# Two-bank exp groups and a third shared PSUM bank in the opening of an attention and gated-MLP block

## The chip, the cores and the metric

The kernel runs on one core of one Trainium2 chip. The metric is the device time in microseconds of one launch. Before the change the median of three runs is 854.6 us (853.17 to 856.5); the profiled execution has a span of 849.3 us from its first to its last instruction. A core has five engines that run their own instruction streams and meet at semaphores: TensorE (PE in the profile), VectorE (DVE), ScalarE (ACT), GpSimd (POOL) and SyncE (SP), which here issues the transfers. Matmul results go to PSUM, eight banks of 128 partitions by 512 float32 values.

## What is computed

One transformer block with conditioning, batch 1, 2048 tokens, width 640, 32 heads of 20, hidden width 1536, in bfloat16:

```python
mod = (silu(c) @ w_mod).reshape(1, 6, 1, 640)
sa, ca, ga, sb, cb, gb = (mod[:, i] for i in range(6))
h = layernorm(x) * (1 + ca) + sa
q, k, v = heads(h @ wqkv)                          # 32 heads of 20
p = softmax(q @ k.T * 20 ** -0.5)                  # 32 x 2048 x 2048
x = x + ga * ((p @ v).merge_heads() @ wo)
h = layernorm(x) * (1 + cb) + sb
x = x + gb * (((h @ w_gate) * (h @ w_up)) @ w_down)
```

The 32 × 2048 × 2048 exponentials of the softmax are the bulk of the work that isn't matmul.

## The kernel before

The program is laid out by a list scheduler that runs in Python when the kernel is built. Tasks have an engine, a modelled duration, dependencies and a priority; a PSUM bank or a buffer is taken from a pool (`Slots`) when a task starts and given back when its last user starts. The order that comes out is fixed, and is emitted with semaphore waits. The numbers that steer it (gates, leads, reserves) are constants at the top of the file; nothing is scheduled on the chip itself.

**Heads and score blocks.** Heads are treated in 8 sets of 4. With the queries of one chunk (512, 512, 512, 256 or 256 tokens), a set makes an *item*. A *block* is one head, 128 keys by 512 queries (or two key tiles by 256): one PSUM bank of scores, transposed, keys on partitions. In the first chunk an item has 64 blocks. A block goes one of two ways:

- most blocks go to ScalarE, which reads two or three banks in one exp instruction;
- about one in five goes to VectorE ("D" blocks), which makes the exponential from the bit pattern of the number, four blocks at a time: one instruction per block out of PSUM (line 1244), then three on all four (lines 1272, 1277, 1280).

The ScalarE blocks are numbered in one row and cut into groups that alternate between two bank sets, so that the matmuls of one group run while ScalarE reads the other:

```python
while ap < NA:
    even = len(glist) % 2 == 0
    us = ubuf[ap:ap + (3 if even else 2)]
    apos.append(ap)
    ap += len(us)
    glist.append((us, 0 if even else 3))        # banks 0,1,2 or 3,4
...
def fexp(e, nu=nu, b0=b0, cellp=cellp, g=g):    # line 1220
    return e.activation(PPs[g % 2][:, cellp["p"], 0:nu * 512],
                        ps[:, b0:b0 + nu, :].rearrange("p b c -> p (b c)"), AFT.Exp, scale=ESCALE)
```

**PSUM.** Banks 0 to 4 hold the scores of the two group sets; bank 7 sums probability times value (PV). Banks 5 and 6 are the shared pool `G`: every transpose, every projection, every matmul of the output projection and of the MLP, and every D block takes a bank there and keeps it until VectorE or ScalarE has copied it out. Before the first scores, the score banks are lent:

```python
G = Slots([5, 6], "G")
GX = Slots([2, 3, 4], "GX")        # three of the first five transposes
GC = Slots([0, 1], "GC")           # the first two columns of the modulation, fillers
BPV = 7
```

**The opening.** Tokens come in four blocks `tc` of 512. Each block is normalised by VectorE, transposed and scaled into `hT[tc]`, then projected. A head takes 20 rows, but a set's four heads must lie on partitions 0, 32, 64 and 96. There are two ways to get there:

- *direct* (`kq_round`): five times four matmuls of 32 columns put each head on its place, and one copy fills `KT[:, j, ...]`; one round per head set;
- *packed* (`packed_round`): 128 rows of K or Q at a time, a copy to a staging tile, a write to DRAM, and one read of 32 KB per head (K), or one of a whole set (Q), which spreads the rows. Five rounds of 128 rows cover all eight sets.

```python
K_DIRECT = (0, 1)      # head set 0 direct for these token blocks
K_ALL = (0, 1)         # all head sets direct for these token blocks
...
def k_base(tc):
    return 80 if tc in K_DIRECT else 0
def nblk(tc):
    return -(-(D - k_base(tc)) // 128)
...
for tc in range(4):
    if tc > 0 and tc in K_DIRECT:
        kq_round("K", 0, tc, need(tc / 4))
    for t in range(4 * tc, 4 * tc + 4):
        v_round(t, 0, need(t / 16 + V_L))
...
for tc in range(4):
    for j in range(1, NSET if tc in K_ALL else 0):
        late.append((j + tc / 4 - KD_LEAD, 2560, lambda p, g, ...: kq_round("K", j, tc, p, g)))
    for b in range(0 if tc in K_ALL else nblk(tc)):
        r0 = b * 128 + k_base(tc)
        j0 = max(0 if tc not in K_DIRECT else 1, -(-(r0 - 91) // 80))
        late.append((j0 + tc / 4 - K_LEAD, 2560, lambda p, g, ...: packed_round("K", b, tc, p, g)))
```

**Copies out of PSUM.** An `evac` task belongs to VectorE, but ScalarE may take it until `STEAL_END` nanoseconds of model time, when it has no task of its own due within 0.3 us.

**Exp results** go to two rings `PPs` of four slots each, from which PV matmuls read. D blocks join a score group where a row strip of the array is free: a score matmul uses 32 rows, so up to four heads run side by side, and with three blocks in a group one strip is left (`d_attach`). `D_RES` says how far ahead of a due D block projections leave a shared bank to it. The gates of the later projections and of the MLP are counted in exp groups.

Of the kernel before, what the change touches and what calls it, by code (L numbers as in the profile page):

```python
# [21 lines left out]
T0 = 700.0  # L22
DMA_SLOW = 0.0015
DMA_LAT = 1700.0
STEAL_END = 60000.0
STEAL_GAP = 300.0
HAM_W = 3413.3
HAM_MIN = 2550.0
# [37 lines left out]
class Slots:  # L66

    def __init__(self, ids, name=""):
        self.name = name
        self.free = [(i, []) for i in ids]  # L70
        self.hold = {}

    def avail(self, only=None):
        best = None
# [7 lines left out]
                best = (t, k)  # L82
        return best

    def take(self, k, refs=1):
        i, rel = self.free.pop(k)
        self.hold[i] = [refs, []]
        return i, rel

    def done(self, i, task):  # L90
        h = self.hold[i]
        h[0] -= 1
        h[1] = [x for x in h[1] if x.nbytes or x.eng != task.eng] + [task]
        if h[0] == 0:
            del self.hold[i]
            self.free.append((i, h[1]))

    def add(self, i, rel):
        self.free.append((i, rel))
# [289 lines left out]
QUADS = [(3, 3, 3, 3, 3, 3, 4, 3), 3, (3, 3, 3, 3, 3, 3, 4, 3), (1, 2, 1, 2, 1, 2, 0, 2), 1]  # L389
D_LEAD = 0.35  # L390
NB0, NSS = 2, 3
NPS = 4
TS_4X, TT_2X = 600.0, 1145.0
WM_GATE = 16
WM_NEED = 1.802
K_DIRECT = (0, 1)
Q_DIRECT = 2
K_LEAD = 0.577
K_ALL = (0, 1)
KD_LEAD = 0.431  # L400
DMA_WINDOW = 900000
D_LATE = 12
D_RES = 100
PVMIN, PVMAX, PVCAP = 2, 11, 16
GATE_F = [0.8, 0.95, 0.819, 0.5, 1.0]
FILL_MIN = 4200.0
DUP_MIN = 0.0
XN_POOL = ()
# [4 lines left out]
HT_L = 0.072  # L413
V_L = 0
LATE_A = 1.174
LATE_L = 2.08
LATEQ = (3,)
LATEQ_A = 6
LATEQ_F = 0.73
QUAD_GAIN = 0.597233983857778  # L420
NTERM = 2
# [6 lines left out]
def sb_cost(n, rate):  # L428
    return n * rate + 62.0


def build_kernel(nc, A_x, A_wqkv, A_wo, B_x, B_w_gate, B_w_up, B_w_down, c, w_mod, out):
# [166 lines left out]
            stx.append(C.alloc("stx", [128, 2, KD, 128], BF16))  # L599
        nsq, nsx = nsx, len(stx)  # L600

    G = Slots([5, 6], "G")
    GX = Slots([2, 3, 4], "GX")
    GC = Slots([0, 1], "GC")
    BPV = 7
    setA = Slots([0], "A")
# [14 lines left out]
    def dve(dur, f, deps=(), prio=3.0, **k):  # L621
        return sc.add(Task("dve", dur, f, deps, prio=prio, **k))
# [6 lines left out]
    def pool(dur, f, deps=(), prio=3.0, **k):  # L629
        return sc.add(Task("pool", dur, f, deps, prio=prio, **k))  # L630

    def act(dur, f, deps=(), prio=3.0, **k):
        return sc.add(Task("act", dur, f, deps, prio=prio, **k))
# [111 lines left out]
            self.evac = after(self)  # L745
            self.evac[-1].on_start = lambda task: banks.done(b["b"], task)

    def quarters(n, lhs, rhs, st, sp):
        def one(x):
            return lambda e, b: e.matmul(ps[32 * x:32 * x + 32, b, 0:n], lhs()[:, 32 * x:32 * x + 32], rhs(),  # L750
                                         tile_position=(0, 32 * x), start=st, stop=sp, skip_group_check=True)
        return [one(x) for x in range(4)]

# [2 lines left out]
    def X(n):  # L756
        return max(n / 2.4 + 3.0, 60.0)
# [67 lines left out]
    def hT_rounds(tc, prio):  # L825
        s2 = tc % 2
        t_hT[tc] = []
        tr_last[tc] = []
        for k in range(KD):
            mms = []  # L830
            for i in range(4):
                f = lambda e, b, i=i, k=k: e.transpose(bankh(b)[:, i * 128:(i + 1) * 128],  # L832
                                                       xn[:, s2, i, k * 128:(k + 1) * 128], ident[:])
                mms.append((C128, f))

            def after(r, k=k):
                dst = hT[tc][:, k, :]
                fa = lambda e: e.activation(dst, bankh(r.b["b"])[:, 0:512], AFT.Identity,  # L838
                                            bias=mcol[:, 0, k:k + 1], scale=mcol[:, 1, k:k + 1])
                f = lambda e: e.tensor_scalar(dst, bankh(r.b["b"])[:, 0:512], mcol[:, 1, k:k + 1], mcol[:, 0, k:k + 1],  # L840
                                              op0=ALU.mult, op1=ALU.add)
                return [evac(512, 455, f, fa, [r.last] + ev_col)]
            r = Round(mms, [t_xn[tc][i] for i in range(4)] + [p_id], after, prio, name=f"hT{tc}.{k}",
                      banks=GX if tc == 0 and k in (1, 3, 4) else None)
            t_hT[tc].append(r.evac[0])
            tr_last[tc].append(r.last)

# [208 lines left out]
    ap = 0  # L1056
    apos = []
    while ap < NA:
        even = len(glist) % 2 == 0
        us = ubuf[ap:ap + (3 if even else 2)]  # L1060
        apos.append(ap)
        ap += len(us)
        glist.append((us, 0 if even else 3))
# [126 lines left out]

    score_q = []
    act_tasks = []
    gx_evac = [t_hT[0][k] for k in (1, 3, 4)]
    act_of = {}
    st_pv = {"item": 0, "free": [d_pz]}
    d_state = {}
# [122 lines left out]
    def item_end_tasks(it):  # L1319
        ci, j = items[it]  # L1320
        n = CHUNKS[ci][1]
        nb32 = n // 32
        slot = ci % 2
        cell = {}
        t1 = Task("dve", n * 1.1 + 70, lambda e: e.transpose(OT[:, 0:n], ps[:, BPV, 0:n]), [], prio=0.0, name=f"T1.{it}")  # L1325
        t1.acq = [(sOT, "o", 1)]
        item_info[it]["t1"] = t1
        t2 = dve(155, lambda e: e.reciprocal(invT[:, 0:nb32].unsqueeze(2),
                                            OT[:, 0:n].rearrange("p (b c) -> p b c", c=32)[:, :, 0:1]), [t1], prio=1.5)
        t3 = dve(sb_cost(n, 1.04), lambda e: e.tensor_tensor(  # L1330
            OTn[:, 0:n].rearrange("p (b c) -> p b c", c=32), OT[:, 0:n].rearrange("p (b c) -> p b c", c=32),
            invT[:, 0:nb32].unsqueeze(2).to_broadcast([128, nb32, 32]), ALU.mult), [t2], prio=1.5)
        t4 = dve(n * 1.1 + 65, lambda e: e.transpose(OcT[:, cell["s"], 0:n], OTn[:, 0:n]), [t3], prio=1.5)
        pcs = oc_pieces(j) if j < NSET - 1 else []
        t4.acq = [(sOcT, "s", max(1, len(pcs)))]

        def on4(task):
            cell["s"] = task.slots["s"]
            sOT.done(0, task)
        t4.on_start = on4  # L1340
        dms = []
        for (b5, s, r0, nr, ro) in pcs:
            def f(e, b5=b5, s=s, r0=r0, nr=nr, ro=ro):
                return e.dma_start(Ocp[r0:r0 + nr, slot, b5, 0:n],
                                   OcT[32 * s + 1 + ro:32 * s + 1 + ro + nr, cell["s"], 0:n])
            dps = [t4] + ([z_oc[slot]] if b5 == KD - 1 else [])
            if ci >= 2:
                dps += oc_free[ci - 2]
            else:
                dps += [x for l in tr_last.values() for x in l]  # L1350
            t = dma("sp", nr * n * 2, f, dps, prio=2, dur=720.0)
            t.on_start = lambda task: sOcT.done(cell["s"], task)
            dms.append(t)
        oc_ready.setdefault(ci, []).extend(dms)
        if j == NSET - 1:
            oc_ready[ci].append(t4)
            oc_last[ci] = cell
        sc.left += 1
        t1.seq = 0
        return t1  # L1360
# [5 lines left out]
    def suffix(ci):  # L1366
# [88 lines left out]
        for fc in range(FT):  # L1455
            use_x = tail and fc < nsx
            wbuf, dm = [], []
            for w_, wv in enumerate((wgv, wuv)):
# [15 lines left out]
                wbuf.append(cell)  # L1474
                dm.append(t)
            gs = fc % 2
            for w_ in range(2):
                mms = []
                for k in range(KD):
# [63 lines left out]
    def acquire_ready(task, t):  # L1543
        for d in task.deps:
            if d.done is None or d.done + SEM > t:
                return False
        return sc.acquire(task, t)
# [132 lines left out]
            st_pv["item"] += 1  # L1680

    tail_added = [False]

    def d_wants():
        g = pvstate["sidx"]
# [77 lines left out]
    def pick_pe(t):  # L1763
        sc.pull("pe")
        g = pvstate["sidx"]
        if g < NG:
            ts, us = score_q[g]
            if acquire_ready(ts, t):
                start = mode_start("S", t)
                rows = {}  # L1770
                for u in us:
                    rows[u.s] = rows.get(u.s, 0) + 1
                d_attach(ts, t, apos[g], rows, 2, False)
                dur = 216.0 * max(rows.values()) * clk()
                area = 128.0 * sum(rows.values())
                if sc.recent(t) + area < DUP_MIN and sc.free_at["act"] > start + 2 * dur + 100:
                    ts.emits = ts.emits + ts.emits
                    dur *= 2
                    area *= 2
                    sc.ndup += 1  # L1780
                sc.activity(start, area)
                sc.finish_issue(ts, start, dur)
                pvstate["sidx"] += 1
                just_s[0] = True
                sc.pe_mode = "S"
                sc.pe_end = start + dur
                sc.free_at["pe"] = sc.pe_end
                return True
# [14 lines left out]
        elif not tail_added[0]:  # L1803
            tail_added[0] = True
            la = [a for a in act_tasks[-2:]]
            if all(a.done is not None for a in la):
                for b in range(5):
                    G.add(b, la)
            else:
                tail_added[0] = False  # L1810
        if sc.recent(t) < FILL_MIN and ring() >= RINGLOW and pick_x(t):
            return True
        if XFIRST and ring() >= XFIRST and pick_x(t):
            just_s[0] = False
            return True
        cands = pv_candidates(t, PVCAP)
        it = st_pv["item"]
# [100 lines left out]
```

The softmax here doesn't subtract the row's maximum and nothing guards it: scores larger than these inputs give would overflow.

## Time and profile before

| what | value |
|---|---|
| time, median of three | 854.6 us |
| span of the profiled run | 849.3 us |
| first exp starts, last exp ends | 17.46 us, 814.0 us |
| exp instructions | 335 of three banks (mean 1523 ns), 335 of two banks (mean 1101 ns) |
| D blocks, first instruction | 372, 682 ns each, on VectorE |
| PE, DVE, ACT busy | 793.9, 719.6, 778.7 us |
| granted TensorE clock, whole run | 0.982 |

How to read it. "Busy" is the time in which an engine has an instruction in execution; matmuls overlap in the array, so a busy TensorE is not TensorE at its peak, and the durations of overlapping matmuls add up to more than their busy time. A group line names the source line, the engine and operation, what is written from what with shapes, the count, then busy time and the mean of one, and after the last bar the idle time just before such instructions with what ended it. In an order-of-time listing, consecutive alike instructions are merged (x5), and the first shape stands for all; the note in brackets is the idle time ahead and its releaser. "Clock" is the share of full TensorE speed that was granted. Idle time of an engine that is not the bound costs nothing.

### The profile page before, as it was taken

The numbers are of one execution on the slowest core, as the hardware profiler recorded it, in microseconds if no ns is written. First come the engines' busy times: TensorE is split into PE (matmuls) and PEld (weight loads), VectorE is DVE, ScalarE is ACT, GpSimd is POOL, SyncE is SP. The second block draws the span as 40 slices with busy tenths as digits, with TensorE's granted clock in tenths as the row PEclk, the third lists the DMA queues.
The fourth block names the chain that finished last, engine by engine and source line by source line (L and its number), as shares of the span: only waits on it lengthen the run. The fifth ranks groups of instructions, "written<-read, shape, count | busy, mean of one in ns | idle before, by whom it ended". The sixth has DMA issues, their size and how long they took to land.

```text
span 849.3 us, 28015 instructions
## 1 busy us (share of the span) xinstructions
PE 793.9 (93%) x12239; PEld 306.9 (36%) x12239; DVE 719.6 (85%) x1271; ACT 778.7 (92%) x700; POOL 30.6 (4%) x65
## 2 busy tenths in 40 slices
PE   8899999999998999999989999998999999999898
PEld 4432333322223222223323223232344443454477
DVE  7769988899999989898889999889789979677773
ACT  4568899999999999999999999999999999999931
POOL 2300000000001000000001000000011000000000
PEclk9989999999999999999999999999999999999999
DMA  9135222012240122310210122000300236115420
GB/s 296 37 97 158 61 68 58 7 44 76 75 124 18 33 60 57 109 57 13 68 40 6 24 65 56 14 12 14 70 33 6 59 76 135 38 46 113 105 59 20
DMA packets 114433, 53.19 MB, mean 63 GB/s; under 512 B 83359, under 2 KB 114311, under 8 KB 114311
## 3 DMA queue, kind: packets, MB, share of 16 engines
q1 hardware_dynamic: 113383, 50.25, 23.2%
q8 instruction: 97, 1.59, 0.8%
q10 hardware_dynamic: 928, 1.15, 0.4%
q14 instruction: 25, 0.20, 0.1%
HBM read 41.09 MB, written 7.99 MB: 58 GB/s over the span
## 4 chain that ended last, share of the span: by engine, by line
PE 38%; ACT 35%; DVE 16%; issue 11%; POOL 0%; ACTq 0%; DVEq 0%
ACT PP L1220 34%; PE ps_all L750 14%; PE ps_all L1186 11%; PE ps_all L1616 8%; DVE DB L1244 5%; DVE DSS L1277 2%; PE ps_all L917 1%; DVE st L805 1%; DVE DSS L1272 1%; DVE st L1420 1%; DVE xck L1410 1%; PE ps_all L832 1%; DVE wd L1174 1%; PE ps_all L1845 1%; DVE OT L1325 1%
## 5 line engine op out<-in xcount | busy, mean ns | idle before, releaser
L1220 ACT ACTIVATE PP<-ps_all 128x1536 bf16<-128x1536 f32 (+1 forms) x671 | 763.0, 1311 | 17.3 <-PE ps_all L1186 14.7
L1186 PE MATMUL ps_all<-QT,KT 32*128 32x512 bf16 (+1 forms) x2560 | 311.9, 342 | 32.1 <-ACT PP L1220 25.0
L1244 DVE TENSOR_SCALAR DB<-ps_all 128x512 int16<-128x512 f32 x372 | 250.4, 682 | 60.8 <-PE ps_all L1186 59.0
L1186 PEld LDWEIGHTS ps_all<-QT,KT 32*128 32x128 bf16 x2560 | 82.3, 91 | 269.8 <-ACT PP L1220 189.4
L1616 PE MATMUL ps_all<-PP,Vf 128*32 128x512 bf16 (+2 forms) x2112 | 166.3, 347 | 0.4 <-DVE OT L1325 0.2
L1277 DVE TENSOR_TENSOR DSS<-DB,DSS 128x2048 bf16<-128x2048 bf16 x93 | 112.2, 1207 | 0.0
L750 PE MATMUL ps_all<-h2T,stg 128*32 128x512 bf16 x1440 | 109.8, 382 | 1.2 <-DVE DB L1244 0.6
L1616 PEld LDWEIGHTS ps_all<-PP,Vf 128*32 128x32 bf16 (+1 forms) x2112 | 48.1, 94 | 87.9 <-issue 78.2
L1616 PE MATMUL ps_all<-DSS,Vf 128*32 128x512 bf16 (+2 forms) x896 | 75.5, 348 | 0.3 <-DVE DSS L1280 0.2
L1280 DVE TENSOR_SCALAR DSS<-DB 128x2048 int16<-128x2048 int16 x93 | 63.3, 681 | 2.1 <-PE ps_all L1616 2.1
L1272 DVE TENSOR_SCALAR DSS<-DB 128x2048 int16<-128x2048 int16 x93 | 63.3, 681 | 1.6
L750 PE MATMUL ps_all<-wd,hprod 128*32 128x320 bf16 x1152 | 56.2, 302 | 1.2 <-DVE DB L1244 0.7
L750 PEld LDWEIGHTS ps_all<-h2T,stg 128*32 128x32 bf16 x1440 | 33.2, 95 | 37.4 <-issue 15.4
L750 PE MATMUL ps_all<-wo,Ocp 128*32 128x320 bf16 x640 | 34.1, 301 | 1.5 <-DVE DB L1244 1.1
L750 PEld LDWEIGHTS ps_all<-wd,hprod 128*32 128x32 bf16 x1152 | 27.1, 96 | 20.6 <-issue 10.2
L1485 DVE CAST gsb<-ps_all 128x512 bf16<-128x512 f32 (+1 forms) x48 | 29.5, 614 | 3.9 <-PE ps_all L750 3.7
L1325 DVE STREAM_TRANSPOSE OT<-ps_all 128x512 f32<-128x512 f32 (+1 forms) x40 | 24.2, 605 | 10.1 <-PE ps_all L1616 9.8
L917 PE MATMUL ps_all<-hT,wq 128*32 128x512 bf16 x375 | 29.8, 395 | 2.1 <-DVE DB L1244 0.9
L1423 POOL TENSOR_SCALAR sd<-mv 128x1 f32<-128x1 f32 x14 | 6.3, 446 | 707.0 <-DVE mv L1422 707.0
L1616 PEld LDWEIGHTS ps_all<-DSS,Vf 128*32 128x32 bf16 (+1 forms) x896 | 24.5, 96 | 19.2 <-issue 8.0
L750 PE MATMUL ps_all<-wV,hT 128*32 128x320 bf16 x640 | 29.9, 312 | 0.9 <-ACT hT L838 0.3
L1496 DVE TENSOR_TENSOR hprod<-ps_all,gsb 128x512 bf16<-128x512 f32 x36 | 24.6, 683 | 5.4 <-PE ps_all L750 5.1
(108 smaller groups left out, 518.8 us busy)
## 6 DMA issues: line engine op xcount, KB each, us to landing
stg<-in_B_w_gate_dram SPq DMA_DIRECT2D x50, 160.0 KB, 2.5
stg<-in_B_w_up_dram SPq DMA_DIRECT2D x50, 160.0 KB
QT<-q_rows SPq DMA_DIRECT2D x22, 128.0 KB, 2.4
wm<-in_w_mod_dram SPq DMA_DIRECT2D x3, 800.0 KB
x<-in_A_x_dram SPq DMA_DIRECT2D x7, 320.0 KB
KT<-k_rows SPq DMA_DIRECT2D x64, 32.0 KB, 1.9
xck<-in_A_x_dram SPq DMA_DIRECT2D x3, 640.0 KB, 4.2
wd<-in_B_w_down_dram SPq DMA_DIRECT2D x1, 1920.0 KB
```

Of the source, the lines that this page charges most:

```text
L750: return lambda e, b: e.matmul(ps[32 * x:32 * x + 32, b, 0:n], lhs()[:, 32 * x:32 * x + 32], rhs(), tile_position=(0, 32 * x), start=st, s ...
L917: f = [lambda e, b_, k=k, x=x: e.matmul(ps[x:x + min(32, w - x), b_, :], wx[:, k, r0 + x:r0 + min(x + 32, w)], hT[tc][:, k, :], tile_posit ...
L1186: ems.append(lambda e, i=i, kt=kt: e.matmul(dstf()[:, i * u.n:(i + 1) * u.n], KT[32 * u.s:32 * u.s + 32, u.j, kt * 128:(kt + 1) * 128], QT ...
L1220: return e.activation(PPs[g % 2][:, cellp["p"], 0:nu * 512], ps[:, b0:b0 + nu, :].rearrange("p b c -> p (b c)"), AFT.Exp, scale=ESCALE)
L1244: return e.tensor_scalar(DB0[:, st_["slot"], x * 512:(x + 1) * 512], bank(cell["b"]), EBIAS, 0.0, op0=ALU.add, op1=ALU.max)
L1272: return e.tensor_scalar(DSS[:, st_["ss"][0], :], DB0[:, st_["slot"], :], 0x7F, 0x3F00, op0=ALU.bitwise_and, op1=ALU.bitwise_or)
L1277: return e.tensor_tensor(d, DB0[:, st_["slot"], :].bitcast(BF16), d, ALU.mult)
L1280: return e.tensor_scalar(DSS[:, st_["ss"][1], :], DB0[:, st_["slot"], :], 0x7F80, 2, op0=ALU.bitwise_and, op1=ALU.bitwise_or)
L1325: t1 = Task("dve", n * 1.1 + 70, lambda e: e.transpose(OT[:, 0:n], ps[:, BPV, 0:n]), [], prio=0.0, name=f"T1.{it}")
L1485: f = lambda e: e.tensor_copy(gsb[:, gs, 0:n], ps[:, r.b["b"], 0:n])
L1496: f = lambda e: e.tensor_tensor(hprod[:, fc, 0:n], ps[:, r.b["b"], 0:n], gsb[:, gs, 0:n], ALU.mult)
L1616: ems.append(lambda e, i=i, kt=kt, stt=stt, stp=stp: e.matmul(ps[32 * s:32 * s + mc, BPV, 0:u.n], Vf[:, (kt * H + 4 * u.j + s) * VW:(kt * ...
```

## The change

It has four parts.

1. *The first 60 exp groups take two banks each* (banks 0, 1 and banks 3, 4). Later groups alternate three and two as before.
2. *Bank 2 joins the shared pool* `G` until group 59 has been issued; then it is retired from the pool, and group 60 waits for its last user. During the opening, transposes, projections and D blocks have three banks.
3. *K of head set 0 is direct for all four token blocks.* The packed blocks of tokens 1024 to 2047 begin at row 80; there are still five of them.
4. *The plan is refitted*: ScalarE may take copies until 94.9 us in place of 60, and leads, gates, the reserve for D blocks and the limit of PV blocks in one turn have other values.

Three more switches come with it and are off (`GU_ONE`, `XCONT`, `T3_POOL`); they change nothing.

```diff
-STEAL_END = 60000.0
+STEAL_END = 94936.728
@@ class Slots
+    def retire(self, i):
+        self.gone.add(i)
+        for k, (j, rel) in enumerate(self.free):
+            if j == i:
+                self.out[i] = self.free.pop(k)[1]
+                break
@@ in done()
-            self.free.append((i, h[1]))
+            if i in self.gone:
+                self.out[i] = h[1]
+            else:
+                self.free.append((i, h[1]))
@@ constants
+HEADG = 60
+HEAD_OUT = 1
-WM_GATE = 16
-WM_NEED = 1.802
-K_DIRECT = (0, 1)
+WM_GATE = 18
+WM_NEED = 1.721
+K_DIRECT = (0, 1, 2, 3)
-K_LEAD = 0.577
+K_LEAD = 0.567
-KD_LEAD = 0.431
+KD_LEAD = 0.559
-D_RES = 100
-PVMIN, PVMAX, PVCAP = 2, 11, 16
-GATE_F = [0.8, 0.95, 0.819, 0.5, 1.0]
+D_RES = 92
+PVMIN, PVMAX, PVCAP = 2, 11, 18
+GATE_F = [0.8, 0.893, 0.938, 0.5, 1.0]
-LATE_L = 2.08
+LATE_L = 2.164
-LATEQ_A = 6
+LATEQ_A = 7
@@ PSUM
-    G = Slots([5, 6], "G")
-    GX = Slots([2, 3, 4], "GX")
+    G = Slots([5, 6, 2] if HEADG else [5, 6], "G")
+    GX = Slots([3, 4] if HEADG else [2, 3, 4], "GX")
+    hx = (1, 3) if HEADG else (1, 3, 4)
...
@@ groups
-        us = ubuf[ap:ap + (3 if even else 2)]
+        us = ubuf[ap:ap + (3 if even and len(glist) >= HEADG else 2)]
@@ pick_pe
+        if HEADG and g >= HEADG - HEAD_OUT and 2 not in G.gone:
+            G.retire(2)
         if g < NG:
             ts, us = score_q[g]
-            if acquire_ready(ts, t):
+            if HEADG and g == HEADG and 2 in G.out:
+                ts.deps = ts.deps + G.out.pop(2)
+                back[0] = True
+            if (g != HEADG or not HEADG or back[0]) and acquire_ready(ts, t):
...
```

More of the change, by code (lines that the diff above doesn't have):

```diff
@@ L71, in __init__ @@
         self.hold = {}
+        self.gone = set()
+        self.out = {}
     def avail(self, only=None):
@@ L391 @@
 NB0, NSS = 2, 3
+HEADG = 60
+GU_ONE = 0
+XCONT = 0
+T3_POOL = 0
+HEAD_OUT = 1
 NPS = 4
 TS_4X, TT_2X = 600.0, 1145.0
-WM_GATE = 16
-WM_NEED = 1.802
-K_DIRECT = (0, 1)
+WM_GATE = 18
+WM_NEED = 1.721
+K_DIRECT = (0, 1, 2, 3)
 Q_DIRECT = 2
-K_LEAD = 0.577
+K_LEAD = 0.567
 K_ALL = (0, 1)
-KD_LEAD = 0.431
+KD_LEAD = 0.559
 DMA_WINDOW = 900000
 D_LATE = 12
-D_RES = 100
-PVMIN, PVMAX, PVCAP = 2, 11, 16
-GATE_F = [0.8, 0.95, 0.819, 0.5, 1.0]
+D_RES = 92
+PVMIN, PVMAX, PVCAP = 2, 11, 18
+GATE_F = [0.8, 0.893, 0.938, 0.5, 1.0]
 FILL_MIN = 4200.0
@@ L746, in __init__, with quarters @@
             self.evac[-1].on_start = lambda task: banks.done(b["b"], task)
-    def quarters(n, lhs, rhs, st, sp):
+    def quarters(n, lhs, rhs, st, sp, c0=0):
         def one(x):
-            return lambda e, b: e.matmul(ps[32 * x:32 * x + 32, b, 0:n], lhs()[:, 32 * x:32 * x + 32], rhs(),
+            return lambda e, b: e.matmul(ps[32 * x:32 * x + 32, b, c0:c0 + n], lhs()[:, 32 * x:32 * x + 32], rhs(),
                                          tile_position=(0, 32 * x), start=st, stop=sp, skip_group_check=True)
@@ L843, in hT_rounds @@
             r = Round(mms, [t_xn[tc][i] for i in range(4)] + [p_id], after, prio, name=f"hT{tc}.{k}",
-                      banks=GX if tc == 0 and k in (1, 3, 4) else None)
+                      banks=GX if tc == 0 and k in hx else None)
             t_hT[tc].append(r.evac[0])
@@ L1192, in build_kernel @@
     act_tasks = []
-    gx_evac = [t_hT[0][k] for k in (1, 3, 4)]
+    gx_evac = [t_hT[0][k] for k in hx]
     act_of = {}
@@ L1329, in item_end_tasks @@
                                             OT[:, 0:n].rearrange("p (b c) -> p b c", c=32)[:, :, 0:1]), [t1], prio=1.5)
-        t3 = dve(sb_cost(n, 1.04), lambda e: e.tensor_tensor(
+        f3 = lambda e: e.tensor_tensor(
             OTn[:, 0:n].rearrange("p (b c) -> p b c", c=32), OT[:, 0:n].rearrange("p (b c) -> p b c", c=32),
-            invT[:, 0:nb32].unsqueeze(2).to_broadcast([128, nb32, 32]), ALU.mult), [t2], prio=1.5)
+            invT[:, 0:nb32].unsqueeze(2).to_broadcast([128, nb32, 32]), ALU.mult)
+        if T3_POOL and it < len(items) - 1:
+            t3 = pool(n * 2.2 + 200, f3, [t2], prio=0)
+        else:
+            t3 = dve(sb_cost(n, 1.04), f3, [t2], prio=1.5)
         t4 = dve(n * 1.1 + 65, lambda e: e.transpose(OcT[:, cell["s"], 0:n], OTn[:, 0:n]), [t3], prio=1.5)
@@ L1476, in suffix, with after, off @@
             gs = fc % 2
+            if n <= 256 and GU_ONE:
+                mms = []
+                for w_ in range(2):
+                    for k in range(KD):
+                        f = quarters(n, lambda k=k, cell=wbuf[w_]: cell["t"][:, k, :], lambda k=k: h2T[:, k, 0:n],
+                                     k == 0, k == KD - 1, w_ * n)
+                        mms.append((X(n), f))
+                def after(r, gs=gs, fc=fc):
+                    f = lambda e: e.tensor_copy(gsb[:, gs, 0:n], ps[:, r.b["b"], 0:n])
+                    fa = lambda e: e.copy(gsb[:, gs, 0:n], ps[:, r.b["b"], 0:n])
+                    ds = [r.last] + ([g_use[gs]] if gs in g_use else []) + sc_use
+                    if tail:
+                        eg = act(n / 1.2 + 60, fa, ds, prio=1e6)
+                    else:
+                        eg = evac(n, ps_cost(n), f, fa, ds)
+                    f = lambda e: e.tensor_tensor(hprod[:, fc, 0:n], ps[:, r.b["b"], n:2 * n], gsb[:, gs, 0:n], ALU.mult)
+                    return [eg, dve(ps_cost(n), f, [r.last, eg] + (first if alt else bd.get("hp", []) + proj_early + kv_last), prio=1)]
+                r = Round(mms, t_h2 + dm + sfx_done.get("ul", []), after, pr(), gate=gate(2 * KD * n), name=f"u{ci}.{fc}")
+                g_use[gs] = r.evac[1]
+                hp.append(r.evac[1])
+                u_last.append(r.last)
+                if not use_x:
+                    def off(task, wbuf=wbuf):
+                        for w_ in range(2):
+                            sStg[w_].done(wbuf[w_]["i"], task)
+                    r.last.on_start = off
+                continue
             for w_ in range(2):
@@ L1682, in build_kernel @@
     tail_added = [False]
+    back = [False]
     def d_wants():
@@ L1807, in pick_pe @@
                 for b in range(5):
-                    G.add(b, la)
+                    if b != 2 or not HEADG or back[0]:
+                        G.add(b, la)
             else:
@@ L1814, in pick_pe @@
             just_s[0] = False
+            return True
+        if XCONT and xcur[0] is not None and ring() >= XCONT and pick_x(t):
             return True
```

## The prediction, made before the changed kernel was run

> **What bounds the kernel now.** I read the page's engine totals and slices first, then the exp instructions alone by stretch, then all engines in the same stretches, and last the order of time around the one long hole. The totals and the 40 slices of 21.2 us:
>
> ```profile
> PE 793.9 (93%) x12239; PEld 306.9 (36%) x12239; DVE 719.6 (85%) x1271; ACT 778.7 (92%) x700; POOL 30.6 (4%) x65
> ACT  4568899999999999999999999999999999999931
> PEclk9989999999999999999999999999999999999999
> ```
>
> ScalarE (ACT) is full from the sixth slice to the end of the exps. Only the first five slices, some 100 us, and the last two show it below 9. Busy time of the exp line alone, by stretch (columns: from:to in us, length, busy us and count, then clock, DMA share, GB/s):
>
> ```profile
> 17.46:36.00 18.54, 10.72 (x9) 0.95 0.32 90
> 36.00:47.30 11.30, 0.00 (x0) 0.92 0.09 25
> 47.30:60.00 12.70, 10.43 (x9) 0.79 0.48 152
> 60.00:80.00 20.00, 15.14 (x14) 0.87 0.52 154
> 80.00:103.00 23.00, 20.61 (x20) 1.00 0.23 57
> 103.00:814.00 711.00, 706.13 (x622) 0.99 0.22 55
> ```
>
> The first exp starts at 17.46 us and the last ends at 814.0. From 103 us on only 711.0 − 706.1 = 4.9 us are not exp. Before that, 85.5 us of time hold 56.9 us of exp, so 28.6 us are missing. That sum is the whole prize of any change to the opening. ScalarE's other work there (copies out of PSUM) is about 6.2 us, from the engine's 63.1 us busy in all; real idle time is about 22.4 us. The same stretches for all engines (busy us and count of PE, PE weight loads, DVE, ACT, POOL):
>
> ```profile
> 36.00:47.30 11.30, 9.98 (x189) 5.80 (x185) 5.98 (x11) 2.33 (x3) 0.99 (x2) 0.92 0.09 25
> ...
> 80.00:103.00 23.00, 21.85 (x320) 8.89 (x320) 22.56 (x41) 20.61 (x20) 0.00 (x0) 1.00 0.23 57
> ```
>
> In the hole TensorE is busy with projections while both exp-side engines are half empty: a matter of order and latency. By 80 us TensorE (21.9 of 23.0) and VectorE (22.6) are both nearly full, so there a gain needs less work or better packing. What the hole waits for, in order of time (start, length, engine, line):
>
> ```profile
> 29.72 6.12 ACT L1220 ACTIVATE PP<-ps_all 128x1536 bf16<-128x1536 f32 x5 [0.17 <-PE ps_all L1186]
> 39.45 0.69 DVE L926 CAST KPA<-ps_all 128x512 bf16<-128x512 f32 x1 [0.59 <-PE ps_all L917]
> 40.17 0.36 SPq L960 DMA_DIRECT2D k_rows<-KPA  x1
> 41.91 1.71 SPq L973 DMA_DIRECT2D KT<-k_rows  x4
> 47.35 5.59 ACT L1220 ACTIVATE PP<-ps_all 128x1024 bf16<-128x1024 f32 x5 [2.77 <-PE ps_all L1186]
> 47.35 0.34 SPq L960 DMA_DIRECT2D k_rows<-KPA  x1
> 49.51 1.70 SPq L973 DMA_DIRECT2D KT<-k_rows  x4
> ```
>
> Exps stop at 35.84 us, because the K of tokens 0 to 1023 is used up, and start again at 47.35, when K of tokens 1024 to 1535 has been projected, copied out of PSUM at 40.1 us, written to DRAM, read back in four pieces and used for scores at 46.9. From copy to scores is 6.8 us. The same round trip for the last 512 tokens starts at 47.35 and ends in the wait ahead of the exp of 54.36 us (1.42 us in the order of time).
>
> **What the Trainium skill says.** "DMA: Bandwidth & Descriptors", section "Latency and other measured facts", lays most of a transfer's fixed cost of about 2 us on the receipt from memory. This agrees: k_rows<-KPA lands 1.7 us after issue and KT<-k_rows 1.9 us (medians of the DMA issues), and this chain has two in series. "ScalarE: Activation LUTs", "Rules for kernel authors", budgets about 0.3 us per ACTIVATE plus 0.83 ns per element. The trace has two exp forms:
>
> ```profile
> L1220 ACT ACTIVATE PP<-ps_all 128x1536 bf16<-128x1536 f32 x335 | 510.3, 1523 | 12.0 <-PE ps_all L1186 9.4 <-PE ps_all L1616 2.1
> L1220 ACT ACTIVATE PP<-ps_all 128x1024 bf16<-128x1024 f32 x335 | 368.9, 1101 | 5.3 <-PE ps_all L1186 5.3
> ```
>
> A third bank costs 1523 − 1101 = 422 ns, or 0.82 ns per column, and the fixed part is 1101 − 2 × 422 = 257 ns: close to the page. "TensorEngine Tiling (Array Packing)", "PSUM Bottleneck", warns that tiling speeds the matmuls but not the emptying of PSUM. That is this opening: 17.46 to 100 us holds VectorE copies of 0.48 to 0.69 us per round against TensorE rounds of 0.7 to 1.1 us, in a pool of two banks. "TensorE: Matmul & The Clock Gate", Part 1, says that a window of about 3.4 us with too little matmul work halves the clock. The trace has a mean clock of 0.59 between 55 and 63 us and 0.79 over 47.3 to 60, soon after the hole; it doesn't show whether the hole is its cause.
>
> **Part by part.**
>
> 1. **K of head set 0 direct.** Tokens 1024 to 2047 get a projection round that copies straight into the K tile, as tokens 0 to 1023 have already. It takes the place of the urgent packed block 0. The packed blocks then begin at row 80 and are still five: (640 − 80)/128 rounds up to 5. So up to the end of head set 1 TensorE has as many rounds as before (direct plus one block, against two blocks), and later two rounds more, 2 × about 1.1 us, with two copies of 0.68 us. Eight reads of 32 KB go. Taken where the packed block ran (TensorE from 38.1 us, copy until 40.1), the direct round lets scores of 0.4 us follow at once and puts the next exp at about 41, against 47.35: **−6.4 us**. The 12 ScalarE blocks of these 512 tokens then last 12 × 0.55 = 6.6 us (half of 1101 ns each), until about 47.6. The direct round for the last tokens, with a copy that ends at 47.3 as its packed block's did, gives exps at about 48.2: some 0.7 of the 1.4 us go as well. Together **−7.1 us**.
> 2. **TensorE has to follow.** What ran between 36 and 63 us must run some 7 us earlier too. TensorE is 93 to 100% busy there, so I don't credit the whole. Work at clock 0.59 for 8 us loses 3.3 us of it; a fuller start may give part of that back. Credit: **−5.5 us** in place of −7.1.
> 3. **Two-bank groups.** The first 60 groups carry 120 blocks in place of 150. Before, 120 blocks were 48 groups, so there are 12 groups more: 12 × 257 ns = **+3.1 us** of ScalarE. Up to 103 us the kernel did 52 groups, 130 blocks, so the 60 groups cover almost exactly the starved stretch; some of the cost lies where ScalarE would wait. Charged: **+2 us**.
> 4. **A third bank in the shared pool**, for transposes, projections and VectorE's own exp blocks. The visible waits for a bank are short (score weight loads after the VectorE block 5.1 us in 13 waits, single waits under 0.9 us elsewhere), but two rounds can be in evacuation while a third fills, and a two-block score group leaves two row strips for VectorE blocks. The idle time of 60 to 103 us is 4.9 + 2.4 = 7.3 us. Estimate: a quarter of it, **−2 us**. Allowing ScalarE to take copies until 95 us in place of 60 goes to the same account: VectorE is 98% busy there, and each copy moved takes 0.69 us off it.
> 5. **The refitted numbers** (gates, reserve, limit of 18 in place of 16 PV blocks) reorder work behind a ScalarE that is already 99.3% full with exp, and the 35 us after the last exp. No term in the arithmetic; ±2 us in the range.
>
> Sum: −5.5 + 2 − 2 = −5.5 us, so 854.6 − 5.5 = **849.1 us**.
>
> **Rivals.** *A: the opening is TensorE-bound, not latency-bound.* Then K arriving early only moves the hole to 55 to 80 us, and the 3.1 us remain: 854 to 858 us. For it: 12.01 of 12.70 us busy at 47.3 to 60. Against it: much of that is at a reduced clock, and the value projections that fill the hole are not all urgent. *B: the third bank and the fuller start also cure the low clock and the 60 to 103 us stretch.* Then 15 of the 22.4 us idle go, less 3.1: about 842 us. For it, all engines have room between 36 and 60 us. Against it, VectorE is at 98% from 80 us on, and the change takes nothing off it but what ScalarE steals. *C: the moved gates upset the saturated stretch*, because smaller groups shift every gate counted in groups, and handing bank 2 back at group 60 makes the score queue wait for a copy. A wait of 1 us once is nothing; a ring of probability buffers that runs empty in several places would cost 5 to 15 us and give 858 to 865. Against it: the plan was refitted with these very numbers.
>
> **Range and chances.** A gain over 2% needs 17 us, three quarters of all real idle time: unlikely. A loss of 17 us needs rival C on a large scale. I choose 839 to 857 us, from a little beyond B to most of A: faster by over 2% 0.06, within 2% 0.91, slower 0.03.
>
> **What would show it.** Step 1: no stretch above 4 us without exps between 36 and 48 us, exps again at about 41, and 56 reads of K in place of 64. Step 2: exp busy over 17.46 to 60 us well above today's 21.2 us. Step 3: about 12 exps more, and total exp time up by about 3 us. Step 4: shorter waits for L1244 and less idle time of ScalarE at 60 to 103. Overall, the last exp should end at about 808.5 us, with some 35 us behind it. I am wrong if K arrives early and the exps still run dry a little later (A), or if exp-free time after 103 us grows far above 4.9 us (C).

## The result, and the profile after

The changed kernel takes 844.12 us, median of four runs (842.52 to 845.03), against 854.28 us before (853.17 to 856.5): a ratio of 0.9876, 95% interval 0.9851 to 0.9901, so 10 us or 1.24% faster. Forecast were 849.1 us, a gain of 5.5. The time lies in the range of 839 to 857; the size of the gain is nearly twice what was worked out. How large it is to within 1 us isn't settled by these few runs: over the 102 executions of the kernel before that were timed beside the experiments the median is 852.9 us, against which the gain is 8.8, and a second series of the changed kernel gave 11.3 (841.05 against 852.37).

The page of the changed kernel, engine totals and ScalarE's row of its 40 slices (now 21.1 us each):

```profile
PE 794.3 (94%) x12268; PEld 306.1 (36%) x12268; DVE 714.1 (85%) x1266; ACT 783.0 (93%) x719; POOL 31.6 (4%) x65
ACT  4788999998999999999999999999999999999931
```

The work is nearly the same; ScalarE reaches 8 and 9 from the third slice on. The exp line (now L1238) alone, in the stretches of the prediction (from:to, length, exp busy us and count, clock, DMA share, GB/s):

```profile
17.46:36.00 18.54, 11.18 (x12) 1.00 0.44 128
36.00:47.30 11.30, 5.61 (x6) 0.86 0.01 1
47.30:60.00 12.70, 8.24 (x9) 0.99 0.66 206
60.00:80.00 20.00, 17.08 (x19) 0.83 0.42 110
80.00:103.00 23.00, 21.89 (x23) 1.00 0.35 82
103.00:200.00 97.00, 96.84 (x86) 1.00 0.13 36
```

Up to 103 us there are 64.0 us of exp in place of 56.9. An exp that crosses a border is counted in both stretches, so the counts of these rows add up to 69 and those of before to 52; taken as one stretch they are 67 and 50. Sixty of the 67 carry two blocks, and the other seven four threes and three twos: 138 blocks in place of 125. In the full stretch of the kernel before a block costs 706.13/(622 × 2.5) us = 454 ns, so 13 blocks are 5.9 us. The last exp ends at 807.84 us instead of 814.0, 6.2 us earlier, and what follows it takes 34.8 us instead of 35.3. So the traces differ by 6.7 us (spans of 842.6 and 849.3), and nearly all of it is won before 103 us. The medians differ by 10.2, since the profiled execution of before took 851.1 us, 3.2 us less than its median.

The order of time on ScalarE shows that the hole isn't gone:

```profile
28.45 5.61 ACT L1238 ACTIVATE PP<-ps_all 128x1024 bf16<-128x1024 f32 x6 [0.29 <-PE ps_all L1204]
...
37.60 5.61 ACT L1238 ACTIVATE PP<-ps_all 128x1024 bf16<-128x1024 f32 x6 [3.00 <-PE ps_all L1204]
43.74 2.85 ACT L856 ACTIVATE hT<-ps_all,mcol 128x512 bf16<-128x512 bf16 x4 [0.53 <-PE ps_all L850]
...
51.74 20.85 ACT L1238 ACTIVATE PP<-ps_all 128x1024 bf16<-128x1024 f32 x22
```

The third token block's exps start at 37.6 us, ten earlier than before. Then there is a new pause without exps, from 43.2 to 51.7 us, before the fourth token block. Before, the one hole was 11.5 us; now two of 3.5 and 8.5 us add up to 12.0. What has changed is what comes around them. After the second pause 22 exps follow without a break, and until 95.6 us only five short pauses, 4.0 us in all; the kernel before ran dry seven times for 9.5 us in all between its hole and 93.9 us. Before the first pause the exps lose 2.2 us less.

### The profile page after: what moved, and what is told of

Its sections match the earlier page's. It is cut to its first block, busy times and chain, and to the rows that moved or that the text cites. A ratio compares the mean times of both kernels' runs of the same rounds, so it can differ in the third digit from the quotient of the medians.

```text
span 842.6 us, 28098 instructions
## 1 busy us (share of the span) xinstructions
PE 794.3 (94%) x12268; PEld 306.1 (36%) x12268; DVE 714.1 (85%) x1266; ACT 783.0 (93%) x719; POOL 31.6 (4%) x65
## 4 chain that ended last, share of the span: by engine, by line
PE 49%; ACT 22%; DVE 20%; issue 8%; POOL 0%; ACTq 0%; DVEq 0%
ACT PP L1238 22%; PE ps_all L768 17%; PE ps_all L1204 15%; PE ps_all L1666 11%; DVE DB L1262 7%; PE ps_all L935 3%; DVE DSS L1295 2%; PE ps_all L883 2%; DVE DSS L1290 1%; DVE st L823 1%; DVE DSS L1298 1%; DVE xck L1432 1%; DVE OT L1343 1%; DVE st L1442 1%; PE ps_all L850 1%
## 5 line engine op out<-in xcount | busy, mean ns | idle before, releaser
L1238 ACT ACTIVATE PP<-ps_all 128x1024 bf16<-128x1024 f32 (+2 forms) x683 | 763.9, 1297 | 11.2 <-PE ps_all L1204 10.3
L1204 PE MATMUL ps_all<-QT,KT 32*128 32x512 bf16 (+1 forms) x2560 | 308.6, 341 | 26.4 <-ACT PP L1238 21.6
L1262 DVE TENSOR_SCALAR DB<-ps_all 128x512 int16<-128x512 f32 x372 | 250.6, 682 | 65.5 <-PE ps_all L1204 63.6
L1666 PE MATMUL ps_all<-DSS,Vf 128*32 128x512 bf16 (+3 forms) x896 | 75.2, 353 | 0.0
```

The source lines that it names most:

```text
L1204: ems.append(lambda e, i=i, kt=kt: e.matmul(dstf()[:, i * u.n:(i + 1) * u.n], KT[32 * u.s:32 * u.s + 32, u.j, kt * 128:(kt + 1) * 128], QT ...
L1238: return e.activation(PPs[g % 2][:, cellp["p"], 0:nu * 512], ps[:, b0:b0 + nu, :].rearrange("p b c -> p (b c)"), AFT.Exp, scale=ESCALE)
L1262: return e.tensor_scalar(DB0[:, st_["slot"], x * 512:(x + 1) * 512], bank(cell["b"]), EBIAS, 0.0, op0=ALU.add, op1=ALU.max)
L1666: ems.append(lambda e, i=i, kt=kt, stt=stt, stp=stp: e.matmul(ps[32 * s:32 * s + mc, BPV, 0:u.n], Vf[:, (kt * H + 4 * u.j + s) * VW:(kt * ...
```

## The experiments

Three theories of where the gain comes from were put against each other: direct K (Theory 1, the prediction's), the third shared bank (Theory 2), and the refitted numbers (Theory 3). Every kernel computes the whole block. Ratios are against the kernel before, on the same chip, with 95% intervals.

### Each part alone

K direct, all else as before:

```diff
-K_DIRECT = (0, 1)
+K_DIRECT = (0, 1, 2, 3)
```

> K of head set 0 direct for all four token blocks, everything else as before. Theory 1 (the prediction's: the DRAM round trip of K is the hole): 5 to 6 us faster than before, exps of the third token block start near 41 us in place of 47.35, the last exp ends near 808. Theory 2 (the shared banks were what delayed the transposes that feed K): at most 2 us faster, and the hole between 36 and 47 us shrinks by less than 4 us. Theory 3 (the refitted numbers do it): within 2 us of before.

Measured: 849.82 us, ratio 0.9976 (0.9957 to 0.9995), 2 us faster by the ratio. Its order of time, first ScalarE's exps, then TensorE around 46 us:

```profile
39.69 5.54 ACT L1238 ACTIVATE PP<-ps_all 128x1024 bf16<-128x1024 f32 x5 [2.62 <-PE ps_all L1204]
47.22 2.93 ACT L856 ACTIVATE hT<-ps_all,mcol 128x512 bf16<-128x512 bf16 x4 [1.99 <-PE ps_all L850]
56.46 5.97 ACT L1238 ACTIVATE PP<-ps_all 128x1536 bf16<-128x1536 f32 x5 [6.31 <-PE ps_all L1204]
```

```profile
46.78 0.40 PE L850 MATMUL ps_all<-ident,xn 128*128 128x128 bf16 x4 [0.81 <-DVE DB L1262]
47.38 0.44 PE L850 MATMUL ps_all<-ident,xn 128*128 128x128 bf16 x4 [0.20 <-DVE DB L1262]
```

The exps of the third block do start at 39.69 us, as worked out (41). But they end at 45.2 and the next come at 56.46: the hole, 11.2 us, has moved by one token block. The transposes of the last block, which K and V of those tokens need, now stand behind VectorE's exp blocks, which came forward together with the scores and hold the shared banks: the transposes wait for them (0.81 and 0.20 us above), and TensorE is busy for only 25.5 of the 30 us from 17 to 47 us. So Theory 1 got its start and not its gain, and Theory 2 got its gain and not its sign, for the pause of 36 to 47 us shrinks to 3.7 us, by far more than 4. The profiled execution is the slowest of the fourteen (856.37 us); that the hole moves isn't peculiar to it, since the trace of the whole change has the pause before the fourth block too.

The two-bank groups with bank 2 shared, K and numbers as before:

```diff
+HEADG = 60
-    G = Slots([5, 6], "G")
-    GX = Slots([2, 3, 4], "GX")
+    G = Slots([5, 6, 2], "G")
+    GX = Slots([3, 4], "GX")
```

> Two-bank groups for the first 60 and bank 2 in the shared pool, with K and all numbers as before. Theory 1: about equal to before, between 2 us slower and 1 us faster (12 more exps cost 3.1 us, less waiting gives 2 to 3 back). Theory 2: 5 us or more faster, because the transposes of the later token blocks end 3 us or more sooner. Theory 3: within 2 us of before.

Measured: 845.44 us, ratio 0.9909 (0.9874 to 0.9943). Theory 2's size, without any direct K. The exps in order of time:

```profile
44.99 20.75 ACT L1238 ACTIVATE PP<-ps_all 128x1024 bf16<-128x1024 f32 x22 [3.41 <-PE ps_all L1204]
69.06 41.74 ACT L1238 ACTIVATE PP<-ps_all 128x1024 bf16<-128x1024 f32 x41 [3.31 <-PE ps_all L1666]
```

With the DRAM round trip still in place they resume at 45.0 us, 2.4 us sooner than before, and then run on with a single break of 3.3 us. The hole itself is still 10.1 us (34.9 to 45.0); the gain lies mostly behind it. The last transposes end at 41.0 us in place of 44.4, 3.4 us sooner, which is Theory 2's reason.

The refitted numbers alone (`STEAL_END`, leads, gates, `D_RES`, `PVCAP` of the change; no two-bank groups, K as before):

> Only the refitted numbers, ScalarE's copies until 94.9 us among them; three-bank groups and packed K as before. Theories 1 and 2: within 2 us of before. Theory 3: 4 us or more faster.

Measured: 858.61 us, ratio 1.007 (1.005 to 1.0089), from 16 of 22 executions; the other six, at 867 to 870 us, were in a slower state with a lower clock (0.960 to 0.964) and are left out. No theory expected a loss. That the numbers are fitted to three banks, and hurt with two, would explain it, but was not tried by itself.

Bank and K together, numbers as before:

> Both structural parts with the numbers of before. Theory 1: 5 to 7 us faster than before. Theory 2: 7 to 10 us faster, more than the sum of the two alone if the third bank only pays where K follows at once. Theory 3: less than half of the whole change's 10 us, so slower than 849 us.

Measured: 847.32 us, ratio 0.9937 (0.9921 to 0.9954): no more than the bank alone, though the intervals overlap. In size this is Theory 1's range, but Theory 1 gave the bank no part in it; Theory 2's 7 to 10 us are missed. The exp line between 103 and 200 us, first of this kernel, then of the bank-alone kernel:

```profile
103.00:200.00 97.00, 93.41 (x83) 1.00 0.12 33
```

```profile
103.00:200.00 97.00, 96.97 (x87) 1.00 0.15 39
```

What direct K wins early on top of the bank, 2.8 us of exp before 103 us, is lost again after it (3.6 us); the K-alone kernel shows the same there (93.14 of 97). With the refitted numbers the whole change has 96.84, as shown above: the numbers close this gap. What opens it is not shown. It is not direct K alone, since the next kernel has the gap without it.

### Is it the bank or the smaller groups, and who needs the bank?

The bank-alone kernel with bank 2 in nobody's pool until group 60:

```diff
-    G = Slots([5, 6, 2], "G")
+    G = Slots([5, 6], "G")
```

> The first 60 groups in two banks, but bank 2 left unused until group 60; K and numbers as before. Theory A (more shared banks are what pays): 1 to 3 us slower than before, from 12 more exps of 257 ns fixed part. Theory B (smaller groups pay, since scores of two blocks are ready sooner and leave a second row strip for a VectorE block): at least 4 of the 7.5 us gain of the bank-alone kernel stay.

Measured: 856.74 us, ratio 1.0044 (1.0024 to 1.0064), 3.7 us slower: the gain is gone, as Theory A has it, and the loss is a little above its 1 to 3 us. But the reason given for a loss isn't in the trace. The exp line as a whole, before and in this kernel, and this kernel between 103 and 200 us:

```profile
sum 849.30, ACT 763.05; mean ACT 95.38
```

```profile
sum 822.54, ACT 763.51; mean ACT 84.83
103.00:200.00 97.00, 93.77 (x84) 1.00 0.15 42
```

Twelve more exps (682 in place of 670) add 0.5 us of time under exps, not 3.1. The trace is 3.4 us longer (852.7 against 849.3), and as much as 3.1 us of that is missing between 103 and 200 us, where the kernel before has 96.83 us of exp. In all traces of this document the time under exps is between 762.3 and 765.7 us, with 30 two-bank groups and with 100: what tells the kernels apart is time without exps.

Between bank 2 idle (1.0044) and shared (0.9909) lie 1.35%, or 11.5 us. All engines between 17 and 47, and 47 and 103 us (busy us and count of PE, PE weight loads, DVE, ACT, POOL; then the clock), bank 2 idle:

```profile
17.00:47.00 30.00, 26.29 (x468) 13.25 (x464) 24.63 (x65) 18.97 (x24) 10.81 (x23) 1.00 0.22 65
47.00:103.00 56.00, 52.91 (x620) 16.33 (x617) 48.03 (x80) 49.20 (x52) 0.00 (x0) 0.88 0.43 120
```

and bank 2 shared:

```profile
17.00:47.00 30.00, 29.45 (x556) 15.97 (x552) 26.95 (x73) 20.03 (x26) 10.47 (x23) 1.00 0.24 72
47.00:103.00 56.00, 54.64 (x698) 17.31 (x690) 54.25 (x90) 52.60 (x55) 0.00 (x0) 0.97 0.49 136
```

In the same first 30 us at the same full clock TensorE gets 556 matmuls done in place of 468, and is busy 98% in place of 88%. These are projections, not scores. The V and K projections of that stretch and the transposes (L850), grouped by line, bank 2 idle:

```profile
L768 PE MATMUL ps_all<-wV,hT 128*32 128x320 bf16 x256 | 11.2, 300 | 0.4 <-ACT hT L856 0.3
L935 PE MATMUL ps_all<-hT,wk 128*32 128x512 bf16 x40 | 2.5, 379 | 0.0
L883 PE MATMUL ps_all<-hT,wk 128*32 128x512 bf16 x40 | 2.5, 379 | 0.0
L850 PE MATMUL ps_all<-ident,xn 128*128 128x128 bf16 x60 | 6.1, 222 | 3.0 <-DVE Vf L1015 1.7 <-ACT hT L856 0.7 <-DVE hT L858 0.6
```

and shared:

```profile
L768 PE MATMUL ps_all<-wV,hT 128*32 128x320 bf16 x300 | 12.4, 300 | 0.0
L935 PE MATMUL ps_all<-hT,wk 128*32 128x512 bf16 x60 | 4.0, 380 | 0.0
L883 PE MATMUL ps_all<-hT,wk 128*32 128x512 bf16 x60 | 3.7, 379 | 0.0
L850 PE MATMUL ps_all<-ident,xn 128*128 128x128 bf16 x60 | 5.3, 221 | 0.3 <-DVE Vf L1015 0.3
```

At 20 matmuls a round these are some two V rounds and two K rounds more by 47 us. The waits show it only to one who looks at every kind of user. Ahead of score weight loads the waits on VectorE's exp block (L1262) are 5.3 us with bank 2 idle and 2.7 us with it shared, from 17 to 103 us. Ahead of the transposes TensorE stands idle for 3.0 us until copies (`Vf`, `hT`) have emptied a bank, and for 0.3 us with bank 2 shared; that is most of its idle time from 17 to 47 us, 3.7 against 0.6 us. What no wait can show is the order itself: it was made when the kernel was built, and a round that found no bank then simply comes later in TensorE's program.

Then bank 2 for one kind of user only, until group 60 (a view of the pool that passes over bank 2 is given to the others):

```diff
 # VectorE's exp blocks alone may take bank 2
-            banks = banks or G
+            banks = banks or GV
 # transposes and projections alone may take bank 2
-            ga = G.avail()
+            ga = GV.avail()
```

> Two-bank groups; bank 2 open to VectorE's own exp blocks alone, while transposes and projections keep banks 5 and 6; K and numbers as before. If the VectorE blocks are what the third bank serves: 5 us or more faster than before, and exp busy over 47.3 to 103 us above 50 us. If the projections are: within 2 us of the kernel whose bank 2 lies idle.

> Two-bank groups; bank 2 open to transposes and projections alone, while VectorE's exp blocks keep banks 5 and 6; K and numbers as before. If the projections are what the third bank serves: 5 us or more faster than before. If the VectorE blocks are: within 2 us of the kernel whose bank 2 lies idle.

Measured: 844.82 us, ratio 0.991 (0.9875 to 0.9945), and 846.78 us, ratio 0.9913 (0.9883 to 0.9943). Either alone brings the whole gain, which neither expectation of a single needy user allowed. The traces show two ways to it. With bank 2 for VectorE's blocks, the waits on them ahead of score weight loads fall to 1.5 us, while the transposes still wait for 2.5 us between 17 and 47 us; with bank 2 for the projections, the transposes wait for 0.4 us and the score loads for 2.8. That the two kinds crowd each other out of two banks, and a third parts them whoever gets it, fits both; it is inferred. With bank 2 for VectorE's blocks only, the projections stand at 47 us where the idle-bank kernel has them, and catch up later, between 47 and 103 us:

```profile
L904 PE MATMUL ps_all<-hT,wk 128*32 128x512 bf16 x116 | 9.2, 383 | 0.2 <-DVE DB L1283 0.2
L956 PE MATMUL ps_all<-hT,wk 128*32 128x512 bf16 x83 | 6.6, 381 | 0.2 <-DVE KPA L965 0.2
```

These are 199 K matmuls, where the idle-bank kernel has 100 in that stretch.

### In the whole change

The whole change with bank 2 idle until group 60:

> The whole change, but bank 2 left unused until group 60. If the shared bank carries the whole change as it carries the bank-alone kernel (11 us between bank 2 idle and bank 2 shared there): 8 to 13 us slower than the whole change, 852 to 857 us. If direct K and the numbers give their own part here: below 849 us.

Measured: 858.00 us, ratio 1.0063 (1.0042 to 1.0085), against 0.9876 with the bank: 1.9%, or 16 us. That is a little beyond the 8 to 13 us expected. Direct K and the numbers without the bank are worse than the kernel before. Its exps between 47.3 and 60 us:

```profile
47.30:60.00 12.70, 0.00 (x0) 0.60 0.01 1
```

The hole has moved here as in the K-alone kernel, and the clock falls to 0.60 with it.

The whole change with K of tokens 1024 to 2047 packed as before:

> The whole change with K of head set 0 packed as before for tokens 1024 to 2047. If direct K adds its 6 us on top of the bank: 849 us or slower. If the hole is only moved by direct K, because TensorE and VectorE have the same preparation to do either way: within 2 us of the whole change (844 us).

Measured: 844.82 us, ratio 0.9904 (0.9868 to 0.994): within 1 us of the whole change's 844.12, and 2.4 us behind it by the ratios, whose intervals overlap. Direct K does not add 6 us. With the bank and without direct K the numbers add nothing either (0.9909 with those of before).

With ScalarE's copies only until 60 us (`STEAL_END = 60000.0`):

> The whole change with ScalarE taking copies out of PSUM only until 60 us, as before. If the copies of 60 to 95 us matter: 2 us or more slower. If the plan finds other room, or VectorE is no bound once three banks are shared: within 1.5 us of 844. One late copy by ScalarE is seen after 60 us in the whole change's trace, so I expect the second.

Measured: 841.90 us, ratio 0.9867 (0.9835 to 0.99). They bring nothing.

With 30 and with 100 two-bank groups (`HEADG = 30`, `HEADG = 100`):

> The whole change with 30 two-bank groups in place of 60, so that bank 2 goes back to the scores near 65 us. Fixed parts: 6 exps fewer, 1.5 us. If the third bank is worth most while the first items are prepared (to about 60 us): 842 to 846 us. If it works in the whole starved stretch to 100 us: 847 to 851 us, and exps run dry again between 65 and 100 us.

> The whole change with 100 two-bank groups, to about 140 us. ScalarE is full from 80 us on, so nothing is left to win: 8 more exps at 257 ns, 2 us slower than the whole change, 845 to 848 us. If the third bank also keeps the TensorE clock up in the projections of 100 to 140 us: 844 us or less.

Measured: 841.13 us, ratio 0.986 (0.983 to 0.989), and 843.12 us, ratio 0.9889 (0.9857 to 0.9921). The first is below both of its ranges, the second below the 2 us of loss expected: its eight more exps add only 1.1 us to the time under exps (765.0 against 763.9). The length of the stretch hardly matters from 30 groups on, where three-bank groups begin at 63.6 us; the bank has earned its gain by then.

Last, side by side on one chip, the whole change and the bank-alone kernel again, and the whole change with 30 groups and no copies after 60 us:

> The whole change once more, beside the bank-alone kernel on the same chip. If direct K and the numbers give something on top of the bank: 2 us or more faster than the bank-alone kernel beside it, 842 to 845 us. If they give nothing: equal within 1 us.

> Two-bank groups and bank 2 shared, K and numbers as before, once more. If bank and smaller groups are the whole gain: within 1 us of the whole change beside it. Else 845 to 848 us.

> The whole change with 30 two-bank groups and with ScalarE's copies only until 60 us. If both edits save what they seemed to (3 and 2 us) independently: 839 us. If each only was another draw of the plan: 841 to 845 us.

Measured: 841.05 us, ratio 0.9864 (0.9842 to 0.9885); 842.57 us, ratio 0.9888 (0.9855 to 0.9921); 841.91 us, ratio 0.9873 (0.9849 to 0.9896). Whether direct K and the numbers add anything to the bank stays open: 1.5 us by these medians, 2.8 by the ratios of the first series, and both times the intervals overlap. The two edits of the last kernel do not add up to a further gain, and no version was found that clearly beats the changed kernel.

## Why the prediction was right or wrong

**What bounds the kernel**: right. The whole prize lay before 103 us; after it the trace loses as little as before, and some 35 us still follow the last exp. That the last exp ends at 807.84 us, where 808.5 was forecast, is luck: the terms of steps 2 and 4 were wrong in opposite directions.

**Step 1, direct K, and step 2, its credit of −5.5 us**: this failed, not in the latency but in the path. K arrives when worked out (39.69 us in the K-alone kernel) and reads fall from 64 to 56, but K alone is worth 2 us, and on top of the bank nothing that is clear of the noise. The step took the exps to go on once K of the third block was there. They did not: the sign that the prediction gave for being wrong came true, with exps that run dry again from 45.2 to 56.5 us in the K-alone kernel and from 43.2 to 51.7 in the whole change. Rival A named this and was set aside: the hole only moves. In the K-alone kernel its reason, a full TensorE, doesn't hold (25.5 of 30 us busy); the shared banks, which VectorE's blocks held while the last transposes waited, were short. In the whole change TensorE is busy for 28.8 of these 30 us, and the hole moves all the same; what holds the last block there was not tried. Step 2 also read TensorE as 93% busy or more from 36 us on; its own row says 9.98 of 11.30 us, 88%.

**Step 3, two-bank groups, +2 us**: not settled. With the bank idle the kernel is 3.7 us slower (2.0 to 5.5 by the interval), but not by the fixed part of 257 ns. That figure came from the mean durations of exps whose records overlap: 22 two-bank exps in a row take 20.85 us, 0.95 us each, where the mean of one is 1.10; that it came close to the figure it was compared with therefore says little. The forecast sign, about 3 us more of exp time, did not come: 763.9 us in place of 763.05 in the whole change. What the 3.7 us are made of is open: the idle-bank kernel starts its exps 1.0 us later than before (at 18.49 us, as the bank-alone kernel does at 18.53), and it lacks 3.1 us of exp after 103 us.

**Step 4, the third bank, −2 us**: this failed too, and by more: the term is mis-sized by a factor of six. It measures 11.5 us between bank 2 idle and shared, and 16 us in the whole change. The suspicion was right, a pool of two banks for too many users; its price was read in the wrong place. The estimate took a quarter of ScalarE's visible idle time of 60 to 103 us and leaned on the short waits ahead of score weight loads. It left out what the transposes waited for, in the kernel before:

```profile
L832 PE MATMUL ps_all<-ident,xn 128*128 128x128 bf16 x60 | 6.5, 242 | 2.5 <-ACT hT L838 0.8 <-DVE DB L1244 0.6 <-DVE Vf L997 0.6
```

These 2.5 us are part of 3.8 us in which TensorE was idle from 17 to 47 us, outside the stretch that the estimate looked at, and they delay all that is projected afterwards. The bank takes that idle time away (0.6 us in the bank-alone kernel). A second part of step 4, ScalarE's copies until 95 us, is worth nothing.

**Step 5, no term for the numbers**: it depends on the rest. Alone they cost 6 us; with the bank only they do nothing; with bank and K they repair the loss after 103 us, and go from 0.9937 to 0.9876.

Put together by the runs: +3.7 for the smaller groups, −11.5 for the bank, and about −2.8 for K and numbers on top (0.9909 to 0.9876, intervals overlapping), in sum −10.6. The prediction had +2, −2 and −5.5. Its two wrong terms err in opposite directions, and only so did the total come within a factor of two.

**Rival B**, the third bank and a fuller start, came closest, in its 842 us and in its reason; of the higher clock that it also named, the two traces show little (0.982 and 0.986 over the whole run). It was held down by VectorE's 98% between 80 and 103 us. In that stretch the exps rise only from 20.6 to 21.9 us; most of the 7.1 us of exp gained by 103 us lies ahead of it.

## What to carry to other kernels

Where several kinds of work take turns in few PSUM banks, count how long each use holds a bank, from the first matmul to the end of the copy out, and compare that with the banks. Read the waits ahead of every kind of user, and the idle time of the engine that feeds the banks, not only that of the engine that is the bound; in a program of fixed order even these are only part of it. Test a shortage by giving the resource to one user at a time, and by taking it away again while the rest of the change stays. And when a latency is taken out of a chain, ask what the consumers that come forward will occupy, and who stands behind them.

## What the runs showed of the hardware that was not expected

The mean granted TensorE clock of an execution goes with its time within one and the same program. Over 102 executions of the kernel before, from 847.4 to 858.3 us with clocks of 0.970 to 0.990, a straight line gives −4.1 us per 0.01 of clock (correlation −0.90); over 14 of the bank-alone kernel, 839.2 to 849.6 us, −6.2 us (−0.92). So the time of a kernel in which ScalarE is busy nearly all the time still moves with TensorE's clock. The mean clock is 0.979 before, 0.977 with two-bank groups and an idle bank, 0.987 with the bank shared. By the lines at a clock of 0.980, bank idle and shared stand at 856.7 and 848.7 us, so about 8 of the 11.5 us remain at equal clock, and the rest goes together with the higher clock. That the clock is the cause of that rest, and not a mark of the same shortage, was not tried: no run set the clock by itself.
